# A column step of five gaps instead of six, a later inverse stage, and one direct pair fewer between two stretches of block products

## The chip, the cores and the metric

The kernel runs on one core of a Trainium2 chip. The metric is device time in microseconds (us), lower is better. Before the change the median of three runs is 1347.81 us (1347.73 to 1348.21).

The engines are named as the profile names them: PE (TensorE matmuls) and PEld (its weight loads), DVE (VectorE), ACT (ScalarE), POOL (GpSimd) and SP (SyncE, which here only issues DMA transfers). Each engine takes its instructions strictly in the order in which the program lists them.

## The reference

Two mixers of the same input `x` (2048 tokens, 576 features, float32) are blended by a gate per token.

```python
g = sigmoid((x * gate_w).sum(-1, keepdims=True))
X = rfft2(x) * (w_r + 1j * w_i)         # over tokens (2048) and features (576)
a = irfft2(X)
h = gelu(x @ w_gate) * (x @ w_up)       # 576 -> 4608, tanh gelu
b = h @ w_down                          # 4608 -> 576
y = g * a + (1 - g) * b
```

## The kernel before, in words

**The dense half (`b`) fills PE.** Tokens come in two passes of 1024 and the hidden features in 36 blocks of 128; a *pair* is two blocks in one pass, so there are 2 x 18 = 36 pairs. Every float32 operand is split into a high and a low part, and a product of two of them takes three matmuls (high x high, low x high, high x low). `PLAN` names the way in which each of the 36 pairs computes `x @ w_gate` and `x @ w_up`:

- `c`, a **direct pair** (`conv`): eight chains (`chain`, lines 899 to 912) of 14 matmuls of 512 columns, 112 in all.
- `s`, a pair as **block products** (`products`, `seven`): seven products of sums of blocks stand for eight, each 14 matmuls of 512 columns, 98 in all. The sums of the weights (`total`, `prep_b`) are made on DVE and ACT beside it; the sums of `x` for a pass (`operands`) are made once ahead of each stretch of `s` pairs, in the tiles `sx` and `gu`.

In either way 96 matmuls of 288 columns (`down_mm`, line 978) follow for `h @ w_down`; ACT scales each result into `stg`, and a DMA on POOL adds it into `yd` in DRAM (line 991).

`PLAN` before is 2 `c`, 10 `s`, 9 `c`, 15 `s`.

**The spectral half (`a`) is woven in between.** The generator `spectral` makes the two-dimensional transform in stages on DVE and ACT: feature transforms of either half of the tokens (`forward_rows`), the first radix-4 stage over token tiles (`first_tiles`), the **column step** (`columns`), the last inverse radix-4 stage (`last_tiles`, `late_tiles`) and the inverse feature transforms (`inverse_rows`). It needs the tile `til` (16 tiles of 580 columns), whose place in memory is the place of `sx`. So the column step runs in the direct stretch between the two stretches of block products, and `til` must have been written to `bw` in DRAM before `sx` may be made for the second one.

**What sets the order.** All is written out by hand, through `gap()`: at two places in each chain, after each `seven`, and after each `down`. A direct pair has 24 gaps (16 and 8). At a gap the current generator goes on until it yields `None` or until its credit is used up: `tick` adds PE's time to `credit`, a yielded number takes DVE's estimated time off. What stands in `side` (in the column step the small radix-4 butterflies `four`, by the generator `beside`) gets the credit that is left. `at(n, f)` runs `f` n gaps later. `while ops.get("done") != ...` ahead of a stretch of `s` pairs, and `while gens` ahead of the last pair, put in bare gaps until the work is listed.

**The column step before** (lines 320 to 380) runs over `kb` = 0 to 16, with `STEP` = 6 gaps `g` each, as a pipeline over 16 units `Z[kb]` of `til`:

- g = 0: `product(0, kb)`, six matmuls of 290 columns (line 284) into two PSUM banks; SP is told to load the filter for the next unit (`load_ww`, line 260) and four transfers that gather a later unit out of `til` into `near` (`corner(kb + 2, False)`, line 274, which the profile shows as hx<-til); ACT copies the last unit's filtered values `vs` into the high part `yh` (colm<-tmp).
- g = 1: ACT copies one PSUM bank (til<-pone) and the next unit's `xh` (colm<-hx).
- g = 2: DVE combines the banks (`filter_start`, lines 328 and 329); DVE makes the low part `yl` of the last unit (line 277, colm<-tmp,colm).
- g = 3: ACT swaps halves (`swap`); DVE makes the low part `xl` of the next unit (line 277, colm<-hx,colm).
- g = 4: `product(1, kb - 1)` of `yh`, `yl`; ACT copies its banks into `far` (xraw<-pone); DVE multiplies by the filter (lines 371 and 372).
- g = 5: DVE ends the filter (`filter_end`, lines 336 to 338); SP sends `far` back into `til` (`corner(kb - 1, True)`, four transfers, til<-xraw).

For each group of four units, `four` must have run before the gathers, and an inverse `four(d, range(4), sp, 1)` (lines 96, 101, 104) runs once `gone` says that the units of the group have come back; `keep(d)` then stores two of the group's four tiles to `bw`.

After the column step come, still in the direct stretch, `last_tiles(1)` (the last inverse stage for one half of the tokens), twelve loads of `x` for the second pass (`load_xs(1)`), `operands(1)`, and `kept(1)`, which stores that half of `til` in four transfers of 580 KB (line 759). In the last stretch the other half is fetched again (`late_tiles(0)`, `late_tiles(1)`, which end in rows), `inverse_rows(0)` runs, the finished half is fetched (`fetched_rows`), and `inverse_rows(1)` ends the spectral work.

Of the kernel before, what the change touches and what calls it, by code (L numbers as in the profile page):

```python
# [31 lines left out]
STEP = 6  # L32
COLCAP = 2.0
PAIRS = NT // 2
PLAN = "c" * 2 + "s" * 10 + "c" * 9 + "s" * 15
# [53 lines left out]
def _butterfly(eng, full, real, imag, at, sp, sgn, cost):  # L89
# [4 lines left out]
    for o, p, q, op in ((sp, x0, x2, ALU.add), (x0, x0, x2, ALU.subtract), (x2, x1, x3, ALU.add),  # L94
                        (x1, x1, x3, ALU.subtract)):
        eng.tensor_tensor(o, p, q, op)
        yield cost[0]
# [64 lines left out]
def _build(nc, tc, a):  # L162
    with ExitStack() as ctx:
# [74 lines left out]
        def columns():  # L238
# [52 lines left out]
            def beside():  # L291
# [4 lines left out]
                for d in range(3):  # L296
                    while gone[0] < (4 * d + 5) * STEP + 3:
                        yield None
                    yield from four(d, range(4), sp, 1)
                    keep(d)  # L300
                    yield None
# [18 lines left out]
            v = w = None  # L320
            for kb in range(17):
                on, was = kb < 16, 1 <= kb < 17
                if kb < 16:
                    z, (w0, w1) = two(Z[kb]), ww[kb % 2]
                    zr, zi = z[:, 0], z[:, 1]

                def filter_start():
                    vec.tensor_tensor(zi, v[0][:, :NK], zr, ALU.subtract)
                    vec.tensor_tensor(zr, v[0][:, :NK], zr, ALU.add)

                def swap():
                    act.activation(vs2[0:64], z[64:128], AF.Copy, scale=-1.0)
                    copy(vs2[64:128], z[0:64])

                def filter_end():
                    vec.tensor_tensor(z, z, two(vs), ALU.add)
                    vec.tensor_tensor(vs2[:, 0], zr, zi, ALU.add)
                    vec.tensor_tensor(vs2[:, 1], zr, zi, ALU.subtract)

                for g in range(STEP):  # L340
                    if g == 0:
# [6 lines left out]
                        if was:  # L348
                            copy(yh, vs)
                    elif g == 1:  # L350
                        if on:
                            copy(zr, v[1][:, :NK])
                        if kb + 1 < 16:
                            copy(xh, near[(kb + 1) % 2])
                    elif g == 2:
                        if on:
                            filter_start()
                        if was:
                            low(yl, vs, yh)
                    elif g == 3:  # L360
                        if on:
                            swap()
# [17 lines left out]
                    yield None  # L380
            gone[0] = 20 * STEP
# [1170 lines left out]
```

## Time and profile before

| | |
|---|---|
| median of three runs | 1347.81 us |
| the profiled execution | 1348.01 us |
| its span, first to last instruction | 1346.2 us |
| PE busy | 1331.9 us (99%) |
| DVE busy | 1122.2 us (83%) |
| ACT busy | 847.7 us (63%) |
| mean granted TensorE clock | 0.999 |

The profiled execution is 0.20 us above the median, and 1.8 us of it lie outside the span. Times in the profile count from the span's start. By the starts of their matmuls (lines 1221 and 903) the first stretch of `s` pairs begins at 77 us, the direct stretch at 425 us, the last stretch at 808 us. A matmul's busy time is modelled and overlaps that of the next, so what one costs is read from the distance between starts. Line numbers (L978) are those of the kernel before; the names are tiles, so hb<-gl is an instruction that writes `hb` from `gl`.

### The profile page before, as it was taken

How to read it: one execution, taken by the hardware profiler on the slowest of the kernel's cores; microseconds unless marked ns; L12 is line 12 of the kernel's file. 1: busy time of each engine (PE TensorE's matmuls, PEld its weight loads, DVE VectorE, ACT ScalarE, POOL GpSimd, SP SyncE). 2: the span in 40 equal slices, each digit the busy share in tenths (PEclk: the TensorE clock that was granted, in tenths of full speed). 3: DMA queues.
4: the chain of work that ended last, by engine and by line, in shares of the span. 5: the costliest groups of instructions: out<-in, count | busy, mean ns of one | idle time of the engine just before them, and what ended most of it. 6: DMA issues, size and time to landing. Idle time of an engine off the chain costs nothing.

```text
span 1346.2 us, 20091 instructions
## 1 busy us (share of the span) xinstructions
PE 1331.9 (99%) x7339; PEld 1178.5 (88%) x7339; DVE 1122.2 (83%) x1589; ACT 847.7 (63%) x1464; POOL 263.7 (20%) x326
## 2 busy tenths in 40 slices
PE   9999999999999999999999999999999999999998
PEld 7888888888888888888888888888888888888888
DVE  7689999899999678887786857899999589899554
ACT  5776666666665545666664386766766776766762
POOL 0011112122122221222220121211221422122321
PEclk9999999999999999999999999999999999999999
DMA  9667767787667977999995865767766987767897
GB/s 315 197 147 153 150 134 134 181 193 133 116 115 158 228 148 186 207 273 258 295 228 150 277 124 108 198 131 135 134 130 134 183 186 134 135 126 135 147 209 177
DMA packets 111044, 232.21 MB, mean 172 GB/s; under 512 B 13025, under 2 KB 26849, under 8 KB 110305
## 3 DMA queue, kind: packets, MB, share of 16 engines
q0 software_dynamic: 44928, 90.98, 44.8%
q1 hardware_dynamic: 66016, 139.95, 32.2%
q8 instruction: 57, 0.93, 0.3%
q14 instruction: 43, 0.34, 0.1%
HBM read 124.36 MB, written 99.39 MB: 166 GB/s over the span
## 4 chain that ended last, share of the span: by engine, by line
PE 90%; DVE 4%; ACT 3%; DMA 2%; issue 1%; SPq 1%; DVEq 0%; ACTq 0%
PE pdn L978 31%; PE pgu L1221 6%; PE pone L1221 6%; PE pgu L1223 6%; PE pgu L1222 6%; PE pone L1223 6%; PE pone L1222 6%; PE pgu L905 4%; PE pgu L903 4%; PE pgu L904 4%; PE pgu L1224 3%; PE pone L1224 3%; PE pone L284 2%; PE pone L904 1%; PE pone L905 1%; PE pone L903 1%
## 5 line engine op out<-in xcount | busy, mean ns | idle before, releaser
L991 POOL DMA_DIRECT2D yd<-stg x264 | 229.1, 868 | 1013.4 <-ACT stg L1004 808.8
L1004 ACT ACTIVATE stg<-pdn,omg 128x576 f32<-128x576 f32 x276 | 204.2, 740 | 271.8 <-PE pdn L978 268.0
L978 PE MATMUL pdn<-dn,hb 128*128 128x288 f32 x2424 | 355.4, 296 | 2.1 <-ACT hb L217 1.9
L978 PEld LDWEIGHTS pdn<-dn,hb 128*128 128x128 f32 x2424 | 342.7, 189 | 15.1 <-ACT hb L217 2.1
L217 ACT ACTIVATE gu<-wq 64x256 fp32r<-64x256 f32 (+4 forms) x377 | 241.6, 655 | 69.8 <-DVE gu L1186 48.7
L1186 DVE TENSOR_TENSOR gu<-wq,gu 128x768 fp32r<-128x768 f32 x175 | 166.8, 954 | 37.2 <-ACT gu L217 36.6
L978 PE MATMUL pdn<-dn,hx 128*128 128x288 f32 x1008 | 154.9, 295 | 0.0
L978 PEld LDWEIGHTS pdn<-dn,hx 128*128 128x128 f32 x1008 | 143.9, 188 | 4.1
L903 PE MATMUL pgu<-xhi,gu 128*128 128x512 f32 x256 | 100.2, 391 | 1.4 <-DVE gl L960 1.4
L1203 DVE TENSOR_TENSOR wq<-wq 128x768 f32<-128x768 f32 x100 | 95.1, 954 | 6.7 <-ACT gu L217 6.1
L905 PE MATMUL pgu<-xlo,gu 128*128 128x512 f32 x256 | 100.1, 391 | 0.0
L904 PE MATMUL pgu<-xhi,gu 128*128 128x512 f32 x256 | 100.0, 390 | 0.0
L217 ACT ACTIVATE hb<-gl 128x512 fp32r<-128x512 f32 x61 | 38.3, 627 | 44.2 <-DVE gl L960 42.6
L1221 PE MATMUL pgu<-xhi,gu 128*128 128x512 f32 x152 | 59.8, 393 | 2.5 <-ACT pgu L217 2.5
L882 DVE TENSOR_TENSOR dn<-wq,dn 128x576 fp32r<-128x576 f32 x72 | 54.2, 753 | 6.7 <-ACT dn L217 6.7
L1221 PE MATMUL pgu<-sx,gu 128*128 128x512 f32 x152 | 59.6, 392 | 0.0
L1223 PE MATMUL pgu<-xlo,gu 128*128 128x512 f32 x152 | 59.4, 391 | 0.0
L1223 PE MATMUL pgu<-sx,gu 128*128 128x512 f32 x152 | 59.3, 390 | 0.0
L1222 PE MATMUL pgu<-xhi,gu 128*128 128x512 f32 x152 | 59.3, 390 | 0.0
L1222 PE MATMUL pgu<-sx,gu 128*128 128x512 f32 x152 | 59.2, 390 | 0.0
L1224 PE MATMUL pgu<-sx,gu 128*128 128x512 f32 x152 | 59.1, 389 | 0.0
L1221 PE MATMUL pone<-xhi,gu 128*128 128x512 f32 x148 | 58.2, 393 | 0.3 <-ACT pone L217 0.2
(254 smaller groups left out, 2819.8 us busy)
## 6 DMA issues: line engine op xcount, KB each, us to landing
yd<-stg POOLq DMA_DIRECT2D x264, 288.0 KB, 4.9
wq<-ws SPq DMA_DIRECT2D x100, 384.0 KB, 4.5
wq<-wd SPq DMA_DIRECT2D x72, 288.0 KB, 5.3
wq<-wgu SPq DMA_DIRECT2D x20, 640.0 KB, 6.0
colm<-col POOLq DMA_DIRECT2D x32, 256.0 KB, 7.3
misc<-wf SPq DMA_DIRECT2D x16, 290.0 KB, 5.9
hx<-til SPq DMA_DIRECT2D x64, 72.5 KB, 6.7
tmp<-wf SPq DMA_DIRECT2D x16, 290.0 KB, 7.3
```

The costliest lines, as they stand in the source:

```text
L217: act.activation(o, i, AF.Copy)
L903: pe.matmul(ps, w[:, 0, k, c], xhi[tb][:, k], start=k == 0, stop=False)
L904: pe.matmul(ps, w[:, 1, k, c], xhi[tb][:, k], start=False, stop=False)
L905: pe.matmul(ps, w[:, 0, k, c], xlo[tb][:, k], start=False, stop=False)
L978: pe.matmul(ps[half], h[:, l, c], d[:, k, half * HD:(half + 1) * HD], start=part == 0 and n == 0, stop=part == 1 and n == 2)
L991: pl.dma_start(yd[u], o, accum_op=ALU.add)
L1004: put(u, lambda o: act.activation(o.rearrange("p (c k) -> p c k", c=2), v[:, :, 0:HD], AF.Copy, scale=omg[:, u:u + 1]), i == 0)
L1186: vec.tensor_tensor(o, x.rearrange("p (c k) -> p c k", c=3), f(w[:, 256:1024]).rearrange("p (c k) -> p c k", c=3), ALU.subtract)
L1221: pe.matmul(ps, hi, xh[:, t], start=start and t == 0, stop=False, skip_group_check=True)
L1222: pe.matmul(ps, lo, xh[:, t], start=False, stop=False, skip_group_check=True)
L1223: pe.matmul(ps, hi, xl[:, t], start=False, stop=False, skip_group_check=True)
L1224: pe.matmul(ps, tl, xt, start=False, stop=stop, skip_group_check=True)
```

## The change

- `PLAN` becomes 2 `c`, 10 `s`, 8 `c`, 16 `s`: eight direct pairs between, 26 pairs as block products in all. Of the last pair before each stretch, tables derived from the plan (`early`, `gu_of`) follow it.
- `STEP` is 5. `filter_end` and `corner(.., True)` of a unit move from g = 5 to g = 0 of the next step, behind that step's product, filter load and gathers; the copy `yh` moves from g = 0 to g = 1, behind the two copies that stood there. The loop has a short eighteenth round for the last unit.
- `keep(d)` stores all four tiles of a group, one gap after its `four`; `last_tiles`, `into_rows`, `fetched_rows`, `kept` and `load_xs` go. The last inverse stage is made for all four quarters in the last stretch, by `late_tiles(0)` to `late_tiles(3)`, each from four transfers (`fetch`) into places of their own, with the first operations reading those places and the scaled copies written out in the function.
- In the second pass `x` is loaded in parts 1, 2 and 0 around the last `four`; `operands(1)` begins with the sums of part 1 and then waits until `HOLD` = 5 gaps after the last `keep` before anything is written into `sx`.

```diff
-STEP = 6
+STEP = 5
+HOLD = 5
-PLAN = "c" * 2 + "s" * 10 + "c" * 9 + "s" * 15
+PLAN = "c" * 2 + "s" * 10 + "c" * 8 + "s" * 16
...
-            for kb in range(17):
+            for kb in range(18):
...
                     if g == 0:
...
                         if was:
-                            copy(yh, vs)
+                            u = two(Z[kb - 1])
+                            vec.tensor_tensor(u, u, vs2, ALU.add)
+                            vec.tensor_tensor(vs2[:, 0], u[:, 0], u[:, 1], ALU.add)
+                            vec.tensor_tensor(vs2[:, 1], u[:, 0], u[:, 1], ALU.subtract)
+                        corner(kb - 2, True)
                     elif g == 1:
                         if on:
                             copy(zr, v[1][:, :NK])
                         if kb + 1 < 16:
                             copy(xh, near[(kb + 1) % 2])
+                        if was:
+                            copy(yh, vs)
...
-                    elif g == 5:
-                        if on:
-                            filter_end()
-                        if was:
-                            corner(kb - 1, True)
...
+            while count[0] < n + 2:
+                yield None
+            load_part(1, 1)
+            load_part(1, 2)
             while count[0] < n + 4:
                 yield None
             yield from four(3, range(4), sp, 1)
+            yield None
             keep(3)
+            at(1, lambda: load_part(1, 0))
+            kept[0] = count[0]
...
         def keep(d):
-            for e in range(2):
+            for e in range(4):
...
+        def fetch(e):
+            for d in range(4):
+                nc.sync.dma_start(fetched[d], bw[:, SW * (4 * e + d):SW * (4 * e + d + 1)])
...
-            load_xs(1)
...
-            yield from last_tiles(1)
-            yield from with_stores(operands(1), kept(1))
+            yield from operands(1)
             yield from until(3)
+            fetch(0)
+            for _ in range(4):
+                yield None
             yield from late_tiles(0)
             yield from late_tiles(1)
-            fetch(1, 0, places_of[1])
             yield from inverse_rows(0)
-            yield from fetched_rows()
+            for _ in range(4):
+                yield None
+            yield from late_tiles(2)
+            yield from late_tiles(3)
             yield from inverse_rows(1)
...
+                if p == 1:
+                    yield from sums(1)
+                    while count[0] < kept[0] + HOLD:
+                        yield None
```

How the change moves instructions, at three places. First SP's queue in one step of the column step (misc<-wf and tmp<-wf are the filter loads in turn, hx<-til the gathers, til<-xraw the way back, wq<-wgu and wq<-wd the dense half's weights). Before:

```order
L260 DMA misc<-wf 128x580 x2
L274 DMA hx<-til 64x290 x4
L860 DMA wq<-wgu 128x1280
L274 DMA til<-xraw 64x290 x4
L260 DMA tmp<-wf 128x580 x2
L274 DMA hx<-til 64x290 x4
```

and in the changed kernel:

```order
L262 DMA misc<-wf 128x580 x2
L276 DMA hx<-til 64x290 x4
L276 DMA til<-xraw 64x290 x4
L820 DMA wq<-wd 128x576 x2
L262 DMA tmp<-wf 128x580 x2
L276 DMA hx<-til 64x290 x4
L276 DMA til<-xraw 64x290 x4
```

The four transfers back into `til` now stand behind the filter loads and the gathers of the next step; before they stood ahead of them.

Second, ACT's queue in about one step. Before:

```order
L217 ACTIVATE colm<-tmp 128x580
L217 ACTIVATE hb_78<-gl_83 128x512
L217 ACTIVATE til<-pone 128x290
L217 ACTIVATE colm<-hx 128x580
L953 ACTIVATE gl_82<-pgu 128x512
L332 ACTIVATE tmp<-til 64x580
L217 ACTIVATE tmp<-til 64x580
L217 ACTIVATE xraw<-pone 128x290 x2
```

and in the changed kernel:

```order
L219 ACTIVATE til<-pone 128x290
L219 ACTIVATE colm<-hx 128x580
L219 ACTIVATE colm<-tmp 128x580
L357 ACTIVATE tmp<-til 64x580
L219 ACTIVATE tmp<-til 64x580
L219 ACTIVATE hb_78<-gl_83 128x512
L219 ACTIVATE xraw<-pone 128x290 x2
```

The copy colm<-tmp (`yh`), which reads what DVE's end of the filter writes, stood ahead of til<-pone; it now stands behind it and behind colm<-hx.

Third, SP's queue at the end of the direct stretch (yd<-stg stores a first result, bw<-til is `kept` or `keep`, the loads from xs are `x` for the second pass, wq<-ws the weights of the first `s` pair). Before:

```order
L640 DMA bw<-til 128x580 x2
L1072 DMA xraw<-xs 128x512 x4
L1072 DMA tmp<-xs 128x512 x3
L1072 DMA orow<-xs 128x512
L1072 DMA tmp<-xs 128x512 x2
L1072 DMA misc<-xs 128x512 x2
L989 DMA yd_112<-stg_86 128x576
L989 DMA yd_113<-stg_87 128x576
L989 DMA yd_114<-stg_88 128x576
L865 DMA wq<-wd 128x576 x2
L759 DMA bw<-til 128x1160 x4
L1171 DMA wq<-ws 128x768 x4
```

and in the changed kernel:

```order
L1023 DMA tmp<-xs 128x512 x2
L1023 DMA misc<-xs 128x512 x2
L1023 DMA tmp<-xs 128x512 x3
L1023 DMA orow<-xs 128x512
L944 DMA yd_108<-stg_86 128x576
L944 DMA yd_109<-stg_87 128x576
L944 DMA yd_110<-stg_88 128x576
L615 DMA bw<-til 128x580 x4
L1023 DMA xraw<-xs 128x512 x4
L1127 DMA wq<-ws 128x768
```

The stores that `sx` must wait for are four of half the size, eight of the twelve loads of `x` stand ahead of them, and part 0 (xraw) directly behind.

More of the change, by code (lines that the diff above doesn't have):

```diff
@@ L319, in columns @@
             yield None
-            v = w = None
-            for kb in range(17):
+            for kb in range(18):
                 on, was = kb < 16, 1 <= kb < 17
-                if kb < 16:
+                if on:
                     z, (w0, w1) = two(Z[kb]), ww[kb % 2]
                     zr, zi = z[:, 0], z[:, 1]
[L327 to L338, printed above, removed]
                 for g in range(STEP):
@@ L1117, in steps @@
                     high(n, 0)
-                yield from sums(1)
+                if p == 0:
+                    yield from sums(1)
                 for n in raw:
```

120 lines of the change are left out of this document (40 added, 80 removed).

## The prediction, made before the changed kernel was run

> **What bounds the kernel now.** I read the page's chain of waits first, then the waits of PE alone.
>
> ```profile
> span 1346.2 us, 20091 instructions
> PE 90%; DVE 4%; ACT 3%; DMA 2%; issue 1%; SPq 1%; DVEq 0%; ACTq 0%
> ```
>
> ```profile
> PE pgu L1221 <- ACT pgu L217: 2.5, 2, 1.6
> PE pdn L978 <- ACT hb L217: 1.9, 1, 1.9
> PE pgu L903 <- DVE gl L960: 1.4, 1, 1.4
> PE pone L284 <- DVE colm L277: 0.9, 1, 0.9
> ```
>
> Nine tenths of the chain is PE's own work, and the waits (us in total, times, longest) add up to some 7 us. So the time is the number of matmuls times their pitch, plus a handful of waits, each of which can be looked at by itself. Two of the three largest waits of 0.9 us or more behind the first stretch belong to the column step (lines 903 and 284), one (line 978) to the end of the direct stretch. The first row lies in the first stretch of block products, where the change moves nothing; I leave it as it is.
>
> **First term: one direct pair becomes block products.** From the chain of waits in order of time (start, us, what), two starts of the same block, one pair apart, first in the direct stretch outside the column step, then in the last stretch:
>
> ```profile
> 457.02 3.18 PE pdn L978 x24
> ...
> 495.23 3.18 PE pdn L978 x24
> ...
> 1220.29 3.18 PE pdn L978 x24
> ...
> 1255.35 3.18 PE pdn L978 x24
> ```
>
> A direct pair takes 495.23 - 457.02 = 38.21 us, a pair of block products 1255.35 - 1220.29 = 35.06 us. The difference, 3.15 us for 14 matmuls of 512 columns (0.225 us each), is what the new plan takes off. The number of column products and of 288-column matmuls stays. Neither stretch has a wait in these windows, so the term is as firm as the chain: 3.1 to 3.2 us, as long as the work beside PE still fits.
>
> **Second term: the wait at the end of the direct stretch.** Here are PE, ACT and SP around 770 us from the timeline, the transfers issued in that window (KB each, median us to landing), and two windows with the granted clock as the third number from the right:
>
> ```profile
> 772.76 0.95 PE L978 MATMUL pdn<-dn,hb 128*128 128x288 f32 x6
> 775.57 4.38 PE L978 MATMUL pdn<-dn,hb 128*128 128x288 f32 x18 [1.86 <-ACT hb L217]
> 779.78 0.40 PE L903 MATMUL pgu<-xhi,gu 128*128 128x512 f32 x1
> ```
>
> ```profile
> 757.72 1.26 ACT L217 ACTIVATE gu<-wq 128x1280 fp32r<-128x1280 f32 x1
> 769.52 0.63 ACT L217 ACTIVATE sx<-tmp 128x512 fp32r<-128x512 f32 x1 [10.53 <-issue]
> ...
> 774.90 0.61 ACT L217 ACTIVATE hb<-gl 128x512 fp32r<-128x512 f32 x1
> ```
>
> ```profile
> 757.47 3.82 SPq L759 DMA_DIRECT2D bw<-til  x4
> ```
>
> ```profile
> bw<-til SPq DMA_DIRECT2D x4, 580.0 KB, 7.1
> ```
>
> ```profile
> 773.00:775.00 2.00, 0.71 (x6) 0.48 (x4) 0.81 (x2) 2.00 (x5) 0.86 (x1) 1.00 1.19 146
> 776.31:779.72 3.41, 3.41 (x15) 3.41 (x15) 2.14 (x4) 3.31 (x6) 0.00 (x0) 0.50 0.26 47
> ```
>
> ACT stands still for 10.53 us before its first write into `sx`. The page can only say "issue"; since `sx` takes the place of `til`, it is the four stores of 580 KB out of `til`, which SP issues from 757.47 to 761.29 and which take 7.1 us at the median: the last is down at about 761.29 + 7.1 = 768.4, and ACT goes on at 769.52. Behind that copy stand a gelu and the high part `hb` (774.90) that PE's `down_mm` needs, so PE waits 1.86 us. It then runs 3.41 us at half clock. Together 24 matmuls take 779.78 - 772.76 = 7.02 us where the rows above give 3.18 us: a loss of 3.84 us.
>
> In the Trainium skill, the page "TensorE: Matmul & The Clock Gate", section "What's actually happening", the clock falls to half after an idle window of about 3.4 us and comes back after a busy one of the same length. The 3.41 us at 0.50 agree with the second half of that, but a wait of 1.86 us was enough here. By the page's rule so short a wait costs no clock, the gain would be 1.86 us and the dip would come back from another cause; that is a rival below.
>
> The change stores a group as soon as it is done, so that only the last group's four stores of 290 KB come late, and puts `HOLD` = 5 gaps between them and the first write. A gap is 38.21 / 24 = 1.59 us, so five are 8.0 us. SP needs about four times 0.4 to 0.5 us for the four issues, and stores of that size land in
>
> ```profile
> bw<-til SPq DMA_DIRECT2D x6, 290.0 KB, 4.3
> ```
>
> (the transfers issued between 523 and 712 us). That is some 6.3 us against 8.0. ACT should wait little or nothing. What is late next? The loads of `x`: part 0 is issued behind the stores and is first read by DVE at the end of the hold, where 256 KB took
>
> ```profile
> xraw<-xs SPq DMA_DIRECT2D x4, 256.0 KB, 5.0
> ```
>
> so about 1.9 + 2.2 (four issues at 0.55) + 5.0 = 9.1 us after the last `four`, a wait of up to 1.5 us for DVE behind which a product gl<-gl,pone stands. ACT's 10.53 us cost PE 1.86, so 1.5 us on DVE should cost nothing. Bounds: 0 gained (a new wait of the same size) to 3.84; I take 3.5, since both sums come out within a gap of the room given.
>
> **Third term: the column step, six gaps to five.** Its work is the same, laid closer. These rows are DVE's and ACT's largest waits on each other between 523 and 712 us, and the busy times in the column step (PE, PEld, DVE, ACT, POOL; clock, DMA, GB/s):
>
> ```profile
> ACT colm L217 <- DVE tmp L338: 22.0, 11, 3.3
> DVE til L328 <- ACT til L217: 17.9, 11, 2.4
> ```
>
> ```profile
> 523.00:710.00 187.00, 184.70 (x1047) 164.86 (x1047) 153.54 (x252) 115.25 (x197) 45.21 (x62) 1.00 1.02 251
> ```
>
> One step shows how they hang together:
>
> ```profile
> 571.16 0.45 DVE L338 TENSOR_TENSOR tmp<-til 128x290 f32<-128x290 f32 x1
> ...
> 573.83 0.46 DVE L328 TENSOR_TENSOR til<-pone,til 128x290 f32<-128x290 f32 x1 [1.25 <-ACT til L217]
> ...
> 574.70 0.75 DVE L277 TENSOR_TENSOR colm<-tmp,colm 128x580 fp32r<-128x580 f32 x1
> ```
>
> ```profile
> 571.71 0.69 ACT L217 ACTIVATE colm<-tmp 128x580 fp32r<-128x580 f32 x1 [2.76 <-DVE tmp L338]
> ...
> 573.40 0.39 ACT L217 ACTIVATE til<-pone 128x290 f32<-128x290 f32 x1
> ```
>
> ```profile
> 576.91 0.84 PE L284 MATMUL pone<-colm 128*128 128x290 f32 x5
> ```
>
> ACT waits for DVE's end of the filter before it copies `yh`, so til<-pone behind it is late, so DVE waits for til<-pone, so `yl` (line 277) is late for the product at 576.91, with 576.91 - 575.45 = 1.46 us to spare. The spare room is not always that large; a later step has
>
> ```profile
> 665.45 0.75 DVE L277 TENSOR_TENSOR colm<-tmp,colm 128x580 fp32r<-128x580 f32 x1
> ```
>
> ```profile
> 666.51 0.71 PE L284 MATMUL pone<-colm 128*128 128x290 f32 x4
> ```
>
> 0.3 us. The change takes one gap (1.59 us) out of this chain, and by putting til<-pone ahead of `yh` it also takes DVE's wait out, 17.9 / 11 = 1.63 us a step. The two cancel to within 0.1 us, so I expect about the room of before.
>
> Does DVE have the time? It is busy 153.54 of 187.00 us (82%). Sixteen steps lose 16 gaps, but a step that has no credit stretches: written out gap by gap, the changed step loop advances from its first product to its end in seven gaps fewer than before, not sixteen, 7 x 1.59 = 11.1 us. Then DVE has 153.5 in 175.9 us, 87%. DMA moves 251 GB/s; the same bytes and six more stores of 0.29 MB make it about 277, and where the loads of `x` are issued
>
> ```profile
> DMA packets 1452, 2.77 MB, mean 346 GB/s; under 512 B 155, under 2 KB 155, under 8 KB 1451
> ```
>
> it moved 346. Neither is a bound on the mean. Locally the way back is the weak place. Before:
>
> ```profile
> 580.24 2.78 SPq L274 DMA_DIRECT2D til<-xraw  x4
> 583.11 1.43 SPq L260 DMA_DIRECT2D misc<-wf  x2
> 584.59 2.74 SPq L274 DMA_DIRECT2D hx<-til  x4
> ```
>
> ```profile
> til<-xraw SPq DMA_DIRECT2D x56, 72.5 KB, 5.4
> ```
>
> ```profile
> 591.50 0.76 DVE L96 TENSOR_TENSOR til<-til 128x580 f32<-128x580 f32 x1
> ```
>
> The last transfer back lands at about 583.02 + 5.4 = 588.4, and the inverse `four` reads it at 591.50: 3.1 us to spare. Behind filter loads (1.43) and gathers (2.74) it lands 4.2 us later, and one gap less leaves 1.6 us less: 3.1 - 5.8 = -2.7 us, a wait on DVE at each group whose butterfly starts that soon. By the changed order that is one group of the three (in the other two another column product stands before the operation that needs it). DVE's 2.7 us take up the room of `yl`, 0.3 to 1.5 us, and cost PE 1.2 to 2.4 us at the worst. On the other side, the two waits of the column step before (1.4 + 0.9 = 2.3 us) come from DVE being late where the second pass's `x` is prepared beside an inverse `four`; that meeting stays. Bounds for the stretch: all 2.3 us gone, to 2.4 us more at each of the three groups (7.2 us more). I take 0.7 us more, nearest to the one group.
>
> **Fourth term: the inverse stage in the last stretch.** Two more quarters there: six DVE operations of 0.76 us, four of 0.46 each (rows above), up to six of 0.46 for the twiddles and 1.5 us of copies, 10.7 us a quarter, 21 us in all, less some 3 us of the copies it replaces: 18 us. They lie beside PE:
>
> ```profile
> 811.00:1290.00 479.00, 478.78 (x2633) 423.25 (x2632) 420.43 (x565) 327.77 (x577) 106.36 (x126) 1.00 0.74 149
> ```
>
> DVE has 58.6 us free there, and one more pair of 35.06 us. If that cover were gone, 18 us would stand ahead of the last pair. The fetches queue on SP behind a butterfly's reads and ahead of weights for the next pair; I put 0.4 us for the second start of `late_tiles`, from the 0.2 us that PE idles in these 479 us (the first start lies in it), bounds 0 to 1.9.
>
> **Sum.** 1348.01 - 3.15 - 3.5 + 0.7 + 0.4 = 1342.5 for an execution like the profiled one; it is 0.20 above the median, so 1342.3 us. By the page's rule on the clock the second term would be 1.86 - 0.34 = 1.5 and the sum 1344.3.
>
> **The rivals.**
>
> *The wait only moves (1345.8).* ACT or DVE waits for stores or for `x` at the end of the direct stretch and PE stands as long as before: 1342.3 + 3.5. For it: DMA is crowded there (1.19 in the window above), and loads and stores are now closer together. Against it: half the bytes ahead of `sx`, and a hold. Chance 0.14.
>
> *The clock's dip comes anyway (1344.3),* the page's rule. Against it: the dip begins 0.74 us after the wait ends, and nowhere else. Chance 0.04.
>
> *The ways back are late at every group (about 1347).* Three groups of about 2 us in place of 0.7: 1342.3 + 6 - 0.7 = 1347.6 at most. Chance 0.12.
>
> *Each step is late: slower (1351.9).* If the wait that is taken out of DVE's queue comes back in another place (ACT's `yh` behind two copies, the products of the dense half between), the gap of 1.59 us is missing at each of 16 products of `yl`. With a mean room of 1.0 us that is 0.6 us each, 9.6 us: 1342.3 + 9.6. It is slower than before from 0.5 us a step. For it: room of 0.3 us is in the rows. Against it: the 17.9 us. Chance 0.08.
>
> *All waits of the column step go (1339.8).* DVE no longer starts late into the last group: 1342.3 - 0.7 - 1.8. Chance 0.12.
>
> **How the numbers follow.** The forecast has 0.50, with a range of its own of 1340.8 to 1344.5. About 0.2% (2.7 us) is what a measurement of this kernel can tell from no change, so faster is below 1345.1: the forecast, the rival of the clock, the one below and a third of the first, 0.70. Slower, above 1350.5, is the rival of each step with 0.07; the rest is 0.23. The range 1339.8 to 1347.4 leaves out that one, half of the late ways back and a little at the lower end.
>
> **What would show it.** The pairs' distances of 38.21 and 35.06 stay. Right: no wait of PE's line 978 rows for hb at the end of the direct stretch, no window at half clock there, an ACT wait before sx<-tmp of under 3 us; DVE's wait for til<-pone far below 17.9 us, DVE near 87% in the column step; PE waits of 2 to 4 us in that stretch. Wrong: waits of line 284 for colm at many steps; DVE idle ahead of the inverse `four` for transfers; a wait for sx or xraw that PE feels; PE idle in the last stretch beyond 2 us.

## The result and the profile after

The changed kernel takes 1357.23 us (median of 4 runs, 1354.48 to 1357.63) against 1348.01 us for the kernel before on the same chip (1347.73 to 1348.66). The ratio is 1.0063, 95% interval 1.0046 to 1.0081: it is **slower by 9.2 us**, where I forecast 1342.3 us and gave slower a chance of 0.07. The profiled execution took 1357.11 us, with a span of 1355.3 us against 1346.2 before.

To find the place I cut both spans at two products: the first one of the direct stretch and the first block product of the last stretch. The rows are one line's first matmul in a window around it (line, tiles and count: duration min/median/max in ns, first and last start in us). Kernel before:

```profile
L903 PE MATMUL pone<-xhi,gu x1: 398/398/398, 424.8 to 424.8; 128*128 128x512 f32 x1
...
L1221 PE MATMUL pgu<-xhi,gu x1: 389/389/389, 808.5 to 808.5; 128*128 128x512 f32 x1
```

After:

```profile
L858 PE MATMUL pone<-xhi,gu x1: 398/398/398, 425.7 to 425.7; 128*128 128x512 f32 x1
...
L1177 PE MATMUL pone<-xhi,gu x4: 389/389/389, 781.1 to 783.4; 128*128 128x512 f32 x4
```

- Up to the direct stretch: 425.7 - 424.8 = 0.9 us more. The change does nothing there; in the profiles of the eleven kernels below this product starts between 424.7 and 426.0, so it is scatter of single executions.
- The direct stretch: 781.1 - 425.7 = 355.4 us against 808.5 - 424.8 = 383.7. One direct pair (38.21) and the loss at its end (3.84) should have taken off 42.05; it took off 28.3. **So 13.7 us were lost inside it.**
- From there to the end: 1355.3 - 781.1 = 574.2 against 1346.2 - 808.5 = 537.7, 36.5 more where a pair of block products is 35.06: 1.4 lost.

0.9 + 13.7 + 1.4 - 42.05 + 35.06 = 9.0, the 9.1 us between the spans. Here is what PE waits for in the changed kernel between 420 and 800 us (us in total, times, longest):

```profile
PE pone L286 <- DVE colm L279: 6.4, 4, 3.0
PE pone L286 <- ACT colm L219: 2.4, 2, 1.5
PE pgu L1177 <- ACT pgu L219: 1.4, 1, 1.4
PE pone L286 <- ACT xraw L219: 0.6, 3, 0.2
PE pgu L858 <- DVE gl L915: 0.3, 1, 0.3
```

The wait for `hb` at the end of the direct stretch is gone. In its place the column products (line 286) wait 6.4 + 2.4 + 0.6 us, four times as long as all the column step's waits before (1.4 + 0.9). And two of these waits bring half clock with them, 3.41 + 3.42 us after 643.63 and 3.41 us after 722.14 (third number from the right: granted clock):

```profile
643.63:647.04 3.41, 2.39 (x7) 2.13 (x8) 3.38 (x7) 2.09 (x4) 1.27 (x2) 0.50 1.05 157
647.04:650.46 3.42, 3.42 (x12) 3.01 (x11) 3.29 (x6) 0.00 (x0) 0.16 (x1) 0.50 0.99 293
722.14:725.55 3.41, 3.26 (x9) 2.79 (x10) 2.05 (x4) 1.23 (x3) 0.00 (x0) 0.50 0.53 104
```

PE was busy in 2.39 + 3.42 + 3.26 = 9.07 us of these windows (the first number behind the length); half of that is 4.5 us. Waits of 9.7 us with 4.5 of clock, less the 2.3 us of waits before, are 11.9 of the 13.7; the other 1.8 us I have not placed.

The largest single place is at 640 us. PE, DVE and SP from the timeline of the changed kernel:

```profile
641.15 0.53 PE L286 MATMUL pone<-colm 128*128 128x290 f32 x2 [0.85 <-ACT colm L219]
644.65 1.33 PE L286 MATMUL pone<-colm 128*128 128x290 f32 x4 [2.97 <-DVE colm L279]
```

```profile
637.21 1.56 DVE L98 TENSOR_TENSOR til<-til 128x580 f32<-128x580 f32 x2 [6.64 <-DMA til<-xraw]
638.69 0.76 DVE L338 TENSOR_TENSOR til<-til,tmp 128x580 f32<-128x580 f32 x1
...
643.84 0.75 DVE L279 TENSOR_TENSOR colm<-tmp,colm 128x580 fp32r<-128x580 f32 x1
```

```profile
618.18 3.45 SPq L615 DMA_DIRECT2D bw<-til  x4
621.73 0.79 SPq L815 DMA_DIRECT2D wq<-wgu  x1
622.61 2.47 SPq L262 DMA_DIRECT2D misc<-wf  x2
625.17 2.77 SPq L276 DMA_DIRECT2D hx<-til  x4
628.24 4.82 SPq L276 DMA_DIRECT2D til<-xraw  x4
```

Read from below. The ways back of group 1's last column (`til<-xraw`) are issued at 628.24 to 633.06, behind group 0's stores, a filter load and the gathers. DVE has the third operation of that group's inverse butterfly next in its queue, and stands 6.64 us for them. Behind it stand the end of the filter (line 338) and `yl` (line 279), and PE's product waits for those. The chain of waits (start, us, what) tells what the ways back themselves waited for:

```profile
624.21 8.38 DMA misc<-wf
632.60 4.49 DMA til<-xraw
637.21 0.78 DVE til L98
```

By the chain, SP issued the last of them at 632.60, when a filter load landed, 8.38 us after that load had itself been issued. SP did not stand for all of these 8.38 us: the profile shows waits of SP for misc<-wf of 1.4 us in all between 616 and 640, the longest of 1.0. The DMA engines' time by queue in the column step (packets, MB, share of 16 engines' time; 523 to 710 us before, 523 to 726 after) is this, for the kernel before and then after:

```profile
q1 hardware_dynamic: 17947, 29.54, 54.5%
q0 software_dynamic: 8879, 17.28, 46.9%
```

```profile
q1 hardware_dynamic: 19224, 31.47, 53.1%
q0 software_dynamic: 8967, 17.44, 43.3%
...
bw<-til SPq DMA_DIRECT2D x12, 290.0 KB, 5.3
```

54.5 + 46.9 = 101% before, with six stores of 290 KB in the stretch, and 96% after, with twelve. By this count packets were under way on the engines nearly all the time in both kernels, so the mean does not tell them apart.

### The profile page after: what moved, and what is told of

Its sections match the earlier page's. It is cut to its first block, busy times and chain, and to the rows that moved or that the text cites. A ratio compares the mean times of both kernels' runs of the same rounds, so it can differ in the third digit from the quotient of the medians.

```text
span 1355.3 us, 20144 instructions
## 1 busy us (share of the span) xinstructions
PE 1333.7 (98%) x7325; PEld 1177.5 (87%) x7325; DVE 1132.6 (84%) x1612; ACT 855.1 (63%) x1482; POOL 264.1 (19%) x329
## 4 chain that ended last, share of the span: by engine, by line
PE 87%; DMA 4%; ACT 3%; DVE 3%; issue 1%; SPq 1%; DVEq 0%; ACTq 0%
PE pdn L933 30%; PE pgu L1177 6%; PE pgu L1179 6%; PE pgu L1178 6%; PE pone L1177 6%; PE pone L1179 6%; PE pone L1178 6%; PE pgu L1180 3%; PE pone L1180 3%; PE pgu L858 3%; PE pgu L859 3%; PE pgu L860 3%; PE pone L858 1%; PE pone L860 1%; PE pone L859 1%; DMA misc<-wf 1%
## 5 line engine op out<-in xcount | busy, mean ns | idle before, releaser
L933 PE MATMUL pdn<-dn,hb 128*128 128x288 f32 x2388 | 349.4, 295 | 0.0
L933 PEld LDWEIGHTS pdn<-dn,hb 128*128 128x128 f32 x2388 | 336.6, 188 | 12.5 <-DVE hb L919 0.2
L219 ACT ACTIVATE gu<-wq 64x256 fp32r<-64x256 f32 (+3 forms) x389 | 247.9, 651 | 84.6 <-DVE gu L1142 58.6
L1142 DVE TENSOR_TENSOR gu<-wq,gu 128x768 fp32r<-128x768 f32 x182 | 173.2, 953 | 36.6 <-ACT gu L219 35.9
L933 PE MATMUL pdn<-dn,hx 128*128 128x288 f32 x1044 | 161.0, 295 | 0.2 <-DVE wq L1000 0.2
L858 PE MATMUL pgu<-xhi,gu 128*128 128x512 f32 x232 | 92.1, 397 | 0.3 <-DVE gl L915 0.3
L859 PE MATMUL pgu<-xhi,gu 128*128 128x512 f32 x232 | 91.7, 395 | 0.0
L860 PE MATMUL pgu<-xlo,gu 128*128 128x512 f32 x232 | 91.6, 395 | 0.0
L219 ACT ACTIVATE hb<-gl 128x512 fp32r<-128x512 f32 x58 | 36.5, 628 | 47.5 <-DVE gl L915 45.5
L1177 PE MATMUL pgu<-xhi,gu 128*128 128x512 f32 x156 | 61.5, 394 | 3.9 <-ACT pgu L219 3.9
L1177 PE MATMUL pgu<-sx,gu 128*128 128x512 f32 x156 | 61.2, 392 | 0.0
L1177 PE MATMUL pone<-sx,gu 128*128 128x512 f32 x156 | 61.1, 392 | 0.0
L1179 PE MATMUL pgu<-xlo,gu 128*128 128x512 f32 x156 | 60.9, 391 | 0.0
L1179 PE MATMUL pgu<-sx,gu 128*128 128x512 f32 x156 | 60.9, 391 | 0.0
L1179 PE MATMUL pone<-xlo,gu 128*128 128x512 f32 x156 | 60.9, 390 | 0.0
L1179 PE MATMUL pone<-sx,gu 128*128 128x512 f32 x156 | 60.9, 390 | 0.0
L1178 PE MATMUL pgu<-xhi,gu 128*128 128x512 f32 x156 | 60.8, 390 | 0.0
## 6 DMA issues: line engine op xcount, KB each, us to landing
hx<-til SPq DMA_DIRECT2D x64, 72.5 KB, 6.8
```

The lines of the kernel that those rows point to most:

```text
L219: act.activation(o, i, AF.Copy)
L858: pe.matmul(ps, w[:, 0, k, c], xhi[tb][:, k], start=k == 0, stop=False)
L859: pe.matmul(ps, w[:, 1, k, c], xhi[tb][:, k], start=False, stop=False)
L860: pe.matmul(ps, w[:, 0, k, c], xlo[tb][:, k], start=False, stop=False)
L933: pe.matmul(ps[half], h[:, l, c], d[:, k, half * HD:(half + 1) * HD], start=part == 0 and n == 0, stop=part == 1 and n == 2)
L1142: vec.tensor_tensor(o, x.rearrange("p (c k) -> p c k", c=3), f(w[:, 256:1024]).rearrange("p (c k) -> p c k", c=3), ALU.subtract)
```

## The experiments

All are edits of the changed kernel. The kernel before had 1347.06 us beside `back_first`, `back_g4`, `four_later` and `step6`, 1346.65 beside `four1_later`, `keep_late` and the two `four2_end` runs, and 1347.38 beside `keep_pool` and the two `part2_last` runs; the ratios are to these. Beside the changed kernel it had 1348.01, so a difference between an experiment and the change is good to about 1.4 us. Three theories stood against each other: **the queue** (ways back late for one butterfly behind other transfers), **the missing gap** (each `yl` late because a step is shorter), and **crowding** (DVE has too much where a butterfly meets other work).

### Ways back ahead of the filter loads

```diff
                     if g == 0:
                         if on:
                             v = product(0, kb, xh, xl)
+                        corner(kb - 2, True)
+                        if on:
                             load_ww(kb + 1)
                             corner(kb + 2, False)
...
-                        corner(kb - 2, True)
```

> Queue theory: in the changed kernel DVE stood 6.64 us for the ways back til<-xraw of the second group, PE then waited 0.85 + 2.97 us for colm and ran 6.83 us at half clock, 0.85 + 2.97 + 6.83/2 = 7.2 us. Here the ways back are issued ahead of the filter loads and gathers of the same gap. Their two rows ahead, tmp<-wf and misc<-wf, take some 2 to 4 us on the queue, so DVE's wait falls from 6.64 to 3 us or less and PE's wait there to under 1 us without a dip: 1357.2 - 6 = about 1351, between 1349.5 and 1353. Missing-gap theory: the product of yl is late since a step has 1.59 us less, whatever the transfers do; PE still waits 2 us or more for colm near 640 us and the time stays at 1357 +- 1.5.

And one gap earlier still, at the end of the step that made the column:

```diff
-                        corner(kb - 2, True)
...
                             for al in range(2):
                                 copy(two(far[(kb - 1) % 2])[:, al], w[al][:, :NK])
+                            corner(kb - 1, True)
```

> The ways back are issued at the last gap of the same step, one gap earlier than in the changed kernel and right behind the two far copies they carry, so that no filter load of the next step stands ahead of them. Queue theory: they land 3 to 5 us earlier, DVE's wait for til<-xraw goes from 6.64 to under 2 us, the stall of 7.2 us near 640 us goes: about 1350, between 1348.5 and 1352. Missing-gap theory: no change, 1357 +- 1.5. If the issue waits on SP for the far copies and holds up the filter loads behind it, the first product of a step is late instead: PE waits for pone<-colm at many steps, 1357 or more.

Measured: 1362.67 and 1359.86 us, ratios 1.0106 [1.0087, 1.0126] and 1.0093 [1.0069, 1.0118]. Both times were missed. DVE's wait for `til<-xraw` does fall, from 6.6 to 2.1 and 1.6 us, but the gathers, now behind the ways back, come too late for ACT (waits of ACT between 523 and 726 us, first `back_first`, then `back_g4`):

```profile
ACT colm L219 <- DMA hx<-til: 16.0, 3, 10.2
```

```profile
ACT colm L219 <- DMA hx<-til: 15.4, 3, 9.6
```

PE then waits 4.2 + 3.6 us near 680 in `back_first`. So neither of these two orders puts it right: the transfers that now stand second are late in their turn. The queue theory in its simple form, that the ways back only stand in the wrong place, falls.

### Butterflies one step later

```diff
-                    while gone[0] < (4 * d + 5) * STEP + 3:
+                    while gone[0] < (4 * d + 6) * STEP + 3:
```

> The inverse butterfly of each group of 4 waits one step (five gaps, 8 us) longer before it starts; the queue's order is that of the changed kernel. Queue theory: the ways back have 8 us more to land, DVE's wait of 6.64 us goes, PE's stall of 7.2 us near 640 us goes. The groups 0 and 2 move too, so the meeting with other work moves: 1350, between 1348 and 1353. Missing-gap theory: 1357 +- 1.5. If the butterflies pile up behind the last step instead, the last group's stall of 3 + 1.7 us near 720 us grows by a few us, and the gain is given back: 1354 or so.

Measured: 1346.82 us (10 runs), 1.0000 [0.9990, 1.0009]; 10.4 us less than the change, and the same as the kernel before. DVE waits for no way back any more. PE's waits between 420 and 800 us:

```profile
PE pone L286 <- ACT xraw L219: 2.3, 3, 1.2
PE pone L286 <- DVE colm L279: 2.1, 1, 2.1
PE pgu L1177 <- ACT pgu L219: 1.4, 1, 1.4
PE pgu L858 <- DVE gl L915: 0.5, 1, 0.5
```

The DMA engines are as busy as before (55.2 + 45.7% by queue, 257 GB/s between 523 and 712 us), and the twelve stores are in the stretch; the transfers have 8 us more to land. The missing gap by itself is not the cause: the step still has five of them.

The same for group 1 alone:

```diff
-                    while gone[0] < (4 * d + 5) * STEP + 3:
+                    while gone[0] < (4 * d + (6 if d == 1 else 5)) * STEP + 3:
```

> Only the inverse butterfly of group 1 starts one step (five gaps) later; groups 0 and 2 start as in the changed kernel. With all three later the time was 1346.8, 10.4 us under the change. Theory of the one late group: DVE's 6.64 us for til<-xraw, PE's 0.85 + 2.97 us behind it and 6.83 us at half clock are that one group's doing, so this edit alone brings 7 us or a little more: 1350 (1348.5 to 1351.5). Rival, DVE's crowding at each group: each of the three butterflies costs a few us because it meets the low parts yl (the 1.61 us near 596 and the 4.6 us near 720 in the changed kernel), and group 1's share is a third or so: 1353 to 1355.

Measured: 1351.74 us, 1.0039 [1.0026, 1.0052], 5.5 us less than the change: just above the range for the one late group, better than the rival. The stall near 640 is gone, but the late way back turned up at group 2, which has no extra step here. Its DVE, ACT and PE rows:

```profile
682.41 0.76 DVE L98 TENSOR_TENSOR til<-til 128x580 f32<-128x580 f32 x1 [4.81 <-DMA til<-xraw]
```

```profile
683.81 0.63 ACT L219 ACTIVATE hb<-gl 128x512 fp32r<-128x512 f32 x1 [6.79 <-DVE gl L915]
...
686.31 0.73 ACT L959 ACTIVATE stg<-pdn,omg 128x576 f32<-128x576 f32 x1
```

```profile
687.09 3.25 PE L933 MATMUL pdn<-dn,hb 128*128 128x288 f32 x12 [4.47 <-ACT stg L959]
```

DVE waits 4.81 us, a `gl` stands behind the waiting operation, ACT's `hb` waits for that, ACT's copies of `pdn` stand behind `hb`, and PE has no free `pdn`: 4.47 us by a path that never touches the column step. So each butterfly that starts that soon is exposed, and which one is hit depends on what came ahead of it.

### Six gaps again

```diff
-STEP = 5
+STEP = 6
```

> Six gaps a step as in the kernel before, all else as changed. Eight of its gaps no longer fit under the eight direct pairs and stand ahead of the last group of block products with no matmul to cover them; what they cost is not known, 0 to 8 x 1.6 = 12.7 us. Missing-gap theory: the column step's waits (2.4 + 6.4 us in all, with some 5 us of half clock) go back to the 2.3 us of the kernel before, and the pairs between 425 and 700 us run at 38.2 us each: from there the loss is 11 us smaller. Queue theory: the ways back have 1.6 us more per gap, so DVE's wait of 6.64 falls by some 3 us and the stall near 640 us goes as well; so this run tells the two apart only by DVE's wait for til<-xraw and by whether room returns at every step (wait of ACT for DVE's tmp and of DVE for til). The whole: 1346 without a cost of the eight gaps, up to 1359 with it.

Measured: 1366.15 us, 1.0144 [1.0127, 1.0161]. That is above the 1359 that I gave as the upper end: PE waits 11.1 us at the start of the last stretch (for what no longer fits under the direct pairs), and still 5.1 and 2.5 us in the column step. The column products' own waits all but go (0.3 us), so `yl` does get its room back. But the transfers are late as before, and now other results of DVE, behind the waiting butterfly (lines 803 and 915), come late to PE. DVE's waits between 523 and 726 us have the row:

```profile
DVE til L98 <- DMA til<-xraw: 11.7, 3, 7.3
```

With six gaps a step the butterflies wait for the ways back at three places, 11.7 us in all against 6.6 with five. Giving the step its gap back does not cure the late transfers. It does not give the time between issue and use back either: in this run as in the change the last way back of a group is issued at g = 0 and the butterfly let go at g = 3 of the same step, three gaps later, where the kernel before had four (g = 5 to g = 3).

### The stores out of the step loop

```diff
                     yield from four(d, range(4), sp, 1)
                     yield None
-                    keep(d)
...
             load_part(1, 2)
+            for d in range(3):
+                keep(d)
```

> The stores of groups 0 to 2 (twelve of 145 KB) are issued behind the step loop, after the x parts 1 and 2, in place of one group at a time inside it; the butterflies start as in the changed kernel. Rival theory, the stores: group 0's four stores take SP 3.45 us (618.18 to 621.63 in the changed kernel), right ahead of the filter loads, gathers and ways back that group 1 waits for, so without them DVE's 6.64 us falls to 3 us or less, PE's stall near 640 us goes: 1351 +- 1.5. Theory of the start: the butterfly is let go 3 gaps (4.8 us) after ways back that need some 12 to 15 us from there, so the stores make at most 3 us of the 6.6: DVE still waits 3 to 5 us, PE gets back 2 to 4 us at most, 1353 to 1357; the stores behind the loop can cost 1 to 2 us at the end of the direct stretch.

(The twelve stores are of 290 KB each, not of 145.) Measured: 1358.12 us, 1.0086 [1.0069, 1.0103], no better than the change; but the loss has moved. DVE's wait:

```profile
DVE til L98 <- DMA til<-xraw: 2.0, 1, 2.0
```

PE's stall near 640 is gone with it, and the last column product starts at 715.1 in place of 723.2 us: 8.1 us, of which 0.7 lie ahead of the direct stretch. What is gained is lost behind the loop (ACT, then PE):

```profile
749.48 1.15 ACT L219 ACTIVATE sx<-tmp 128x512 fp32r<-128x512 f32 x2 [10.16 <-DMA bw<-til]
```

```profile
751.31 1.84 PE L934 MATMUL pdn<-dn,hb 128*128 128x288 f32 x12 [3.14 <-ACT stg L960]
755.97 2.72 PE L934 MATMUL pdn<-dn,hb 128*128 128x288 f32 x12 [2.82 <-ACT stg L960]
```

That is the wait of the kernel before, come back: ACT's 10.16 us for stores before its first write into `sx` (10.53 there). In the one place the stores cost PE the stall near 640, in the other these two waits of 6.0 us with a window of half clock behind them. That something stands waiting is part of it: `four_later` has the same twelve stores in the loop and no such stall.

The same stores on another queue, at the same gaps as in the change:

```diff
-                nc.sync.dma_start(bw[:, c], til[0][:, c])
+                (pl if d < 3 else nc.sync).dma_start(bw[:, c], til[0][:, c])
```

> The changed kernel with the stores of groups 0 to 2 issued on POOL's queue in place of SP's, at the same gaps. keep_late showed that with these stores out of the step loop DVE's wait for til<-xraw is 2.0 us in place of 6.6 and PE's stall near 640 us is gone. If it was SP's order (3.45 us of issues ahead of the filter loads, gathers and ways back), this run shows the same: DVE's wait at 3 us or less, no stall near 640, 1349 to 1352. If it was the transfers themselves, 1.16 MB more per group for DMA engines whose packets already take 96% of their time (53.1% and 43.3% by queue in this stretch), the wait stays at 5 us or more, the time at 1355 to 1359.

Measured: 1355.9 us, 1.0062 [1.0048, 1.0075], as with the change. DVE's wait falls little, and PE's largest wait there, 2.96 us, stays (the 0.85 us ahead of it is gone, and the profiled execution, with 1353.27 us the shortest of the four, has less half clock):

```profile
DVE til L98 <- DMA til<-xraw: 5.5, 1, 5.5
```

So of what the stores do here, most is done by the transfers and little by SP's order: four issues less ahead of the ways back bring 1.1 us of DVE's wait, no stores in the loop bring 4.6.

### Group 2's butterfly behind the loop

```diff
-                    while gone[0] < (4 * d + 5) * STEP + 3:
+                    while gone[0] < ((4 * d + 6) * STEP + 3 if d < 2 else 20 * STEP):
```

> Groups 0 and 1 one step later (as in the run with all three, 1346.8), and group 2's butterfly behind the step loop, ahead of group 3's. In that run PE still waited 2.09 us for yl at 708.85 and ran some 3 us at half clock, 3.7 us in all, while DVE worked off group 2's butterfly and the second pass's x together. Theory of the crowding: with the butterfly out of that place the 3.7 us go: 1343 (1342 to 1344.5), near the forecast of the prediction. Rival: the work only moves behind the loop, where it delays the last butterfly, the hold and the x sums by its 8 us, and the last direct pair's ACT comes later still (1.4 us at the start of the last stretch becomes 3 to 6): 1346 to 1349.

```diff
+            load_part(1, 0)
             keep(3)
-            at(1, lambda: load_part(1, 0))
```

> As the run before (four2_end), and part 0 of x is issued ahead of the last group's stores in place of behind them. In the run with all three later DVE waited 5.01 us for that part (741.10), and ACT 1.39 us at the start of the last stretch was late for PE. If the late part is what makes ACT late there, PE's wait of 1.39 us falls to 0.3: 1 us less than four2_end. If ACT's own copies ahead of it are, or if ACT now waits for the stores before sx, no change within 1 us, or 1 us more.

Measured: 1347.99 us, 1.0009 [1.0000, 1.0019], and 1346.65 us, 0.9996 [0.9987, 1.0005]. In the profile of the first the crowding is gone: the direct stretch is 344.1 us against 347.1 with all three one step later, and PE waits 0.7 us for `yl` where it was 2.1. But the work behind the loop makes ACT later at the start of the last stretch. The two runs show that wait (PE) and the clock behind it, first `four2_end`, then `four2_end_swap`:

```profile
774.70 0.50 PE L1177 MATMUL pgu<-xhi,gu 128*128 128x512 f32 x1 [2.00 <-ACT pgu L219]
```

```profile
773.41:776.82 3.41, 2.12 (x9) 1.78 (x10) 3.37 (x5) 2.25 (x6) 0.00 (x0) 1.00 0.80 183
```

```profile
773.90 0.50 PE L1177 MATMUL pgu<-xhi,gu 128*128 128x512 f32 x1 [1.83 <-ACT pgu L219]
```

```profile
774.87:778.28 3.41, 3.41 (x9) 2.65 (x9) 1.36 (x2) 1.83 (x4) 0.00 (x0) 0.51 0.06 12
```

2.00 us without a dip, 1.83 us with one. Runs of these two kernels spread over 1345.9 to 1349.8 and 1344.9 to 1347.8. That a dip which comes in some executions makes this spread, I argue; the mean granted clock of every run supports it, though only the two executions have a profile. In `four2_end` the three runs at 1.000 took 1345.9 to 1347.3 us and the seven at 0.998 or 0.999 took 1347.8 to 1349.8; in `four2_end_swap` the clock goes with the time less strictly. The swap's own question stays open: 0.17 us less wait is no answer to either side.

### A version that beats both

`four2_end`, with the part of x that is needed last loaded last:

```diff
             load_part(1, 1)
-            load_part(1, 2)
...
+            load_part(1, 0)
             keep(3)
-            at(1, lambda: load_part(1, 0))
+            load_part(1, 2)
...
                     while count[0] < kept[0] + HOLD:
                         yield None
+                    yield from sums(0)
+                    for n in most:
+                        high(n, 0)
+                    yield None
+                    for n in raw:
+                        high(n, 2)
+                    yield None
+                    for n in most:
+                        low(n, 0)
+                        yield 0.61
...
```

> four2_end with another order at the end of the direct stretch: x part 0 and the last group's stores are issued ahead of part 2 (four times 256 KB that are needed last), and the x sums use part 2 later. In four2_end PE waits 2.00 us for ACT at the start of the last stretch, and the same wait in the swapped run was followed by 3.4 us at half clock. If DVE and ACT come late there because part 0 and the stores land late (DVE 3.86 us for part 0, ACT 5.48 us ahead of its first write into sx in the swapped run), the wait falls below 0.7 us and the half clock goes with it: 1344.5 +- 1, faster than before by 1 to 3 us. If the copies in the last direct pair are simply too many for ACT, the wait stays at 1.4 to 2.4 us: 1346.5 to 1348.

> The run before with a hold of four gaps (6.4 us) in place of five. If the hold is what ends last ahead of the first write into sx, all x sums come 1.6 us earlier: 0 to 1.5 us less than part2_last. If the stores end last, ACT waits up to 1.6 us longer and PE may feel it as in the kernel before: 0 to 3 us more.

Measured: 1345.12 us (11 runs, 1344.76 to 1346.27), 0.9985 [0.9976, 0.9994], and with a hold of four 1345.35 us, 0.9983 [0.9974, 0.9993]. Both are **faster than the kernel before, by 2 us, and so than the change, by some 11**. The time came out as expected, the reason only in part: I expected the wait at the start of the last stretch below 0.7 us, and it is

```profile
PE pgu L1193 <- ACT pgu L219: 1.4, 1, 1.4
```

0.6 us shorter and with the clock at 1.00 behind it. For the rest the row names a copy of ACT; that ACT's copies are simply too many there, the other theory, is not shown. The hold of one gap less changes nothing.

## Why the prediction was wrong, step by step

**What bounds the kernel.** Right: the time is PE's matmuls and a handful of waits, and nearly all that was lost is in PE's waits and the half clock behind them.

**First term, -3.15.** Right. In the last stretch of the changed kernel PE has no idle time (window, us, PE busy first):

```profile
786.00:1325.00 539.00, 539.00 (x2970) 476.96 (x2970) 464.20 (x631) 366.38 (x644) 119.54 (x144) 1.00 0.76 148
```

The part behind the direct stretch is 36.5 us longer, of which 1.39 - 0.22 = 1.2 is the new wait at its start: 35.3 against 35.06. Where no wait lies, the pairs keep their length.

**Second term, -3.5.** The mechanism was right: no wait of line 933 for `hb` at the end of the direct stretch, no half clock there, and ACT waits 0.7 us before `sx`. The size was off by what comes late next. I looked for that at DVE's wait for x part 0, and priced it at up to 1.5 us of DVE and nothing for PE. It is 4.7 us of DVE, and one pair on PE waits 1.39 us at the start of the last stretch, 0.22 before. The term is -3.84 + 1.2 = -2.7. That the late part makes these 1.39 us is not shown: PE's wait is the same with 5.0 us of DVE's (`four_later`) and with 2.6 (`part2_last`).

**Third term, +0.7: the step that failed.** It measured +13.7, above my upper bound of 7.2. The price of the gap itself was right: the 17.9 us that DVE waited for til<-pone fell to 8.0, and no row shows `yl` late at every step, so "each step is late", the rival that came out on the right side of the time (1351.9), did so for a reason that the runs refute: with five gaps and later butterflies the direct stretch is 347.1 us, and 344.1 with group 2's behind the loop, 2.4 above the 383.7 - 42.05 = 341.7 of a stretch that loses no more than before. What failed is what follows on the sentence "Locally the way back is the weak place": the place was right, and its lateness, its price for PE and its bounds were mis-sized. (DVE, forecast near 87% in the column step, was busy in 157.60 of 198.69 us there, 79%: it stood waiting.) The four points:

- I worked the lateness out as 3.1 - 5.8 = -2.7 us, with durations taken from before: 1.43 for the filter issue, 2.74 for the gathers, 2.78 for the ways back. Here these took 2.47, 2.77 and 4.82 us, 3.1 us more, and DVE's wait was 6.64. The longer issue of the ways back comes with the place that the change gives them (the rows below the list).
- I put no price on the four stores that now stand right ahead of group 1's transfers. `keep_late` (DVE's wait 2.0) and `keep_pool` (5.5) show that they make 4.6 of the 6.6 us, most of it by the transfers. The DMA share of 1.02, in the row that I quoted, would not have told: by queue it is 50.1 + 45.7% in `keep_late` without the stores (523 to 716 us), and 55.2 + 45.7% in `four_later`, which has them and no such wait.
- I priced DVE's wait at 1.2 to 2.4 us of PE. It cost 0.85 + 2.97 us of waiting and half of the 2.39 + 3.42 us that PE worked at half clock, 6.7 us (the 7.2 in the expectations counts 0.5 us twice): I had allowed for no clock in this term, though the second term rests on a dip after a wait of 1.86 us.
- I named one group, with all three as a rival (about 1347). One group had the transfer wait in the profile, as I said. The other two cost as well, by DVE's crowding (1.6 us at 596, 1.5 + 1.4 us and a dip near 720), and these were in no bound. The rival had the right place and less than half of the price.

The longer issue of the ways back goes with their standing behind a filter load, and not with the stores. Two such issues, the first in the changed kernel ahead of any store, the second in `keep_late`, which has none in the loop:

```profile
583.62 6.26 SPq L276 DMA_DIRECT2D til<-xraw  x4
```

```profile
623.64 6.52 SPq L276 DMA_DIRECT2D til<-xraw  x4
```

SP's waits for filter loads at the line of the gathers and ways back were 3.9 us before (523 to 712 us) and are 10.2 + 6.6 us in the changed kernel (523 to 726), 9.1 + 6.1 in `keep_late` (523 to 726):

```profile
SPq L274 <- DMA tmp<-wf: 3.9, 4, 1.6
```

```profile
SPq L276 <- DMA misc<-wf: 10.2, 9, 2.1
SPq L276 <- DMA tmp<-wf: 6.6, 6, 1.5
```

**Fourth term, +0.4.** Right, within its bounds (0 to 1.9): nothing is lost in the 539 us quoted, DVE and ACT have the room.

So the sum by measured terms is -3.15 - 2.7 + 13.7 + 0, about +8, and with 0.9 at the start some 8.8 of the +9.1 of the two profiles.

The Trainium skill, "TensorE: Matmul & The Clock Gate", section "What's actually happening", says that the activity window is about 3.4 us and runs freely. The dips here agree in their length, 3.41 us or twice that, and the one wait with a dip and the other without agree with a window that is not tied to the wait. That a whole idle window is needed, as the same section has it, does not agree: a wait of 1.83 us was enough, and one of 0.85 + 2.97 us.

## What to carry to other kernels

Before moving a transfer within a queue, ask what then stands ahead of the one that somebody waits for; the mean share of the DMA engines does not answer that. Here another order or another queue only chose who was late, and the cure was time between issue and use. An engine's wait of a few us must be followed through its queue to PE, and a PE wait near 2 us priced with the 1.7 us of a half-clock window that may follow. A reader that is released at a fixed place of a step has a margin that changes when the issue moves within the step (four gaps before, three after): recompute it in us.

## What the runs showed of the hardware

- SP's issues paused for landings of earlier transfers, as the profile puts it: 16.8 us for filter loads at the line of the gathers and ways back in the changed column step, 3.9 before, and four issues of 72.5 KB took up to 6.52 us there, 2.78 in the step quoted of the kernel before.
- Half clock may or may not follow a wait of this size: 2.00 us without, 1.83 us with 3.41 us at 0.51. Behind 0.85 + 2.97 us it lasted 6.83 us.
- GB/s do not tell how busy the DMA engines are: in the column step 245 to 257 GB/s went with a share of 0.98 to 1.02, while the loads of x reached 346 GB/s at a share of 1.00 (738 to 746 us of the kernel before).
